# Third-sweep matrix sums made in place, block sums between second-stage pieces, and half buffers stored two steps later, in a four-layer attention and Fourier kernel

## Chip, cores and metric

The kernel runs on one NeuronCore of a Trainium2 chip, as one launch. The metric is the device time of an execution in microseconds (us). Before the change, three runs took 1750.28, 1750.65 and 1752.71 us; their median is 1750.65 us.

## What is computed

A sequence of 2048 rows of 640 numbers passes four layers, twice an attention over eight earlier positions and a Fourier mixing. All of it is float32.

```python
def _B_ref(x, dft_seq_re, dft_seq_im, dft_hid_re, dft_hid_im):
    a = jnp.einsum("bsd,ed->bse", x, dft_hid_re)
    b = jnp.einsum("bsd,ed->bse", x, dft_hid_im)
    y = jnp.einsum("ts,bse->bte", dft_seq_re, a) - jnp.einsum("ts,bse->bte", dft_seq_im, b)
    return y
...
x = A_x
x = x + _A_ref(_layernorm(x, axis=-1), A_wqkv, A_wo)
x = x + _B_ref(_layernorm(x, axis=-1), B_dft_seq_re, B_dft_seq_im, B_dft_hid_re, B_dft_hid_im)
x = x + _A_ref(_layernorm(x, axis=-1), A_wqkv, A_wo)
x = x + _B_ref(_layernorm(x, axis=-1), B_dft_seq_re, B_dft_seq_im, B_dft_hid_re, B_dft_hid_im)
```

`_A_ref` is the attention: 32 heads of 20, a window of 8 positions at distance 2.

## The kernel before, in words

A float32 number is held as a high and a low part, both of a type that TensorE multiplies at its full rate, and a product is three matrix multiplies: high by high, high by low, low by high (`PASSES`). ScalarE (ACT) makes the high part by a cast, VectorE (DVE) the low part by a subtraction, which therefore waits for the cast. The pair is called a half here (`half`, L1517).

The Fourier layers multiply first by the sequence matrices and then by the hidden ones. The first of these steps works on eight column groups: the first two by `run`, the other six as three pairs (t1, t2). A pair uses a scheme with seven block products in place of eight: sums of matrix blocks are multiplied by sums of blocks of x. The Fourier layer after the first attention does its pairs in `pair`. The last layer does them in `pairs7`, which this change is mostly about. There every engine but GpSimd executes in the order in which the code is written (`manual_schedule`), so an instruction that waits holds up all that stand behind it on its engine.

`pairs7` goes through 72 steps: 3 pairs, 3 sweeps, 8 steps. At step n:

- `load(n + 2)` issues three loads of matrix blocks (256 KB each) into a ring of seven buffers (`win`, `xa`), and `loadx(n + 2)` two loads of stored block sums of x (256 KB each, `r<-xc`), all in SyncE's (SP's) DMA queue.
- `atoms(n + 2)` puts the pieces of work that make step n+2's halves into a list. `fill` carries them out as long as fewer than six finished halves are held, so the halves run up to six products ahead of TensorE. A piece is a half, and in the first two sweeps sometimes the sum of two matrix blocks as well (`combine`, L1514, a 128x512 addition on DVE). In those two sweeps a sum stands one piece ahead of the half that needs it.
- the products of the step: 18, 21 and 15 matrix multiplies of 512 columns in a step of the first, second and third sweep.

In the third sweep before the change no sum is made at all: the two sums b22-b12 and b11+b12 that it needs had been made in the other Fourier layer, by `ahead_c` in `pair`, and stored there in the DRAM tensor `ccb` by `keep` (L1862: 48 stores of 256 KB). `pre` (L1490) loads them.

Behind the products of a sweep come, in the later pairs, the pieces of the second stage (`v_stage`, L1431) for the column group that is ready: 9, 12 or 21 multiplies of 320 columns each, and a DVE addition of the result to a half row of x (`half[(j, e)]`, 128x320, L1456). Eight such pieces make one column group: three between or behind the steps of a sweep (1, 0, 6), and five behind the last step of the next sweep (2, 3, 5, 4, 7). They share two PSUM banks, `aux0` and `aux1`; a piece that writes on a bank waits until DVE has added what the piece before left in it. `v_evac` makes the operands of the second stage, and `v_run` carries its parts out one by one in the first steps of a sweep, on ACT and DVE.

The half rows have three buffers (`v_halves`): (0,0) and (0,1) share one. A finished half row is put on a list (`pend`) and stored at the next step (`v_flush`). Matrix sums of the second stage, 24 pieces of 160 KB made in the other Fourier layer, are loaded by `v_get` (`wvb`), one at each step of the first pair's second sweep and two at each step of its third.

Of the kernel before, what the change touches and what calls it, by code (L numbers as in the profile page):

```python
# [10 lines left out]
F32 = mybir.dt.float32  # L11
# [15 lines left out]
P = 128  # L27
# [143 lines left out]
)  # L171
NST = 16
# [8 lines left out]
def tile_layers(ctx: ExitStack, tc: tile.TileContext, x, wqkv, wo, cs, cst, wre, wim, out):  # L181
# [50 lines left out]
    ccb = dr.tile([P, NPAIR, NP, 2, 512], F32, name="ccb")  # L232
# [846 lines left out]
    class LayerB:  # L1079
# [276 lines left out]
        def v_halves(self):  # L1356
            xr = T([P, 2, 320], "xr")
            self.half = {(0, 0): xr[:, 0], (0, 1): xr[:, 0], (1, 0): xr[:, 1], (1, 1): T([P, 320], "qs", bufs=2)}
# [62 lines left out]

        def v_load(self, t, je):
            j, e = je
            nc.sync.dma_start(self.half[je], self.xin[t // 2][:, (t % 2) * 2 + j, e * 320 : (e + 1) * 320])

        def v_flush(self):
            for dst, src in self.pend:
                nc.sync.dma_start(dst, src)
            self.pend = []

        def v_stage(self, t, n, tags=("aux0",) * 3 + ("aux1",)):  # L1431
            chain, prod, plain, (j, e) = STAGES[n]
            start = (t, chain) not in self.vb
            if start:
                self.vb[(t, chain)] = pt([P, 512], tags[chain])
            bank = self.vb[(t, chain)]
            mms = []
            if prod:
                for k in KS:
                    for a, b in PASSES:  # L1440
                        mms.append((self.zv[t][(prod[0], k)][a], self.wv[(prod[1], k)][b]))
            if plain:
                pj, pe = plain
                for k in range(len(KS), KD):
                    for a, b in PASSES:
                        for ri in range(2):
                            w = self.wr[:, b, k] if ri == 0 else self.wi[k][b]
                            mms.append(
                                (self.zp[t][k][:, a, ri, pj * P : (pj + 1) * P], w[:, pe * 320 : (pe + 1) * 320])
                            )  # L1450
            for i, (l, r) in enumerate(mms):
                nc.tensor.matmul(  # L1452
                    bank[:, :320], l, r, start=start and i == 0, stop=i == len(mms) - 1, skip_group_check=not start
                )
            h = self.half[(j, e)]
            nc.vector.tensor_tensor(h, bank[:, :320], h, op=ALU.add)  # L1456
            done = self.vl.setdefault(t, [])
            if (j, e) in done:
                self.pend.append((self.xout[t // 2][:, (t % 2) * 2 + j, e * 320 : (e + 1) * 320], h))
            done.append((j, e))  # L1460

        def pairs7(self):
# [18 lines left out]

            def view():
# [7 lines left out]
            def pre(p, i, n):  # L1490
                tag, bufs = wide[self.nraw % len(wide)]
                self.nraw += 1
                raw = T([P, 2, 256], tag, bufs=bufs) if tag != "win" else wtile([P, 2, 256])
                nc.sync.dma_start(raw.rearrange("p r t -> p (r t)"), ccb[:, p, i, n])
                return raw
# [26 lines left out]
            def atoms(n):  # L1522
# [28 lines left out]
                return [lambda k=k, m=m: half(n, m, raws[n][k]) for k, m in enumerate(("c3", "p12", "c6"))]  # L1551
# [37 lines left out]
            for n, (p, sw, i) in enumerate(steps):  # L1589
# [7 lines left out]
                self.v_flush()  # L1597
# [10 lines left out]
                if sw == 0:  # L1608
                    if i == 0:
                        bk["m5"], bk["m4"], bk["m7"] = banks("m0", "m1"), banks("xt", "t0"), banks("t1", "pq")  # L1610
                    if fast:
                        self.v_run((2, 1, 1, 1, 1, 1, 1, 0)[i])
                        if i == 2:
                            self.v_load(tp, (0, 0))
# [10 lines left out]
                    if fast and i == 4:  # L1625
                        self.v_stage(tp, 1)
                    if i < NP - 1:
                        continue
                    (_, m5s), (m4m, m4s), (dm, ds) = store("stg", CFG["bufs"]["stg"]), store("s2"), store("s3")
# [15 lines left out]
                elif sw == 1:  # L1645
# [3 lines left out]
                    if fast:  # L1649
                        self.v_run((0, 1, 1, 1, 0, 0, 0, 0)[i])  # L1650
                        if i == 4:
                            assert not self.todo
                            self.v_load(tp, (0, 1))
                            self.v_load(tp, (1, 1))
                    p11 = h("p11")
# [18 lines left out]
                    for b in range(2):  # L1674
                        combine(ds[b], z(bk["m1"][b]), ds[b], ALU.add)
                    if fast:
                        for k, st in enumerate((2, 3, 5, 4, 7)):
                            self.v_stage(tp, st)
                            if k in (2, 3):
                                fill(1)  # L1680
                    else:
# [3 lines left out]
                        self.v_halves()  # L1685
                        gets += [("t1", k, b) for k in KS for b in range(2)]
                    self.todo = self.v_evac(t1, (dm, m4m), z(bk["f1"][0]))
                else:
# [3 lines left out]
                    if i == 2:  # L1692
                        self.v_load(t1, (0, 0))
                        self.v_load(t1, (1, 0))
                    if i == 7:
# [10 lines left out]
                    if 3 <= i < 6:  # L1706
                        self.v_stage(t1, (1, 0, 6)[i - 3])
# [10 lines left out]
                    for b in range(2):  # L1718
# [12 lines left out]
            self.v_flush()  # L1731
            self.v_run(9)
            t = NT - 1
            for e in range(2):
                self.half[(0, e)] = wtile([P, 320])
            for je in ((0, 0), (1, 0), (0, 1), (1, 1)):
                self.v_load(t, je)
            for n in (1, 0, 6, 2, 3, 5, 4, 7):
                self.v_stage(t, n, ("m0", "m1", "aux0", "aux1"))
                self.v_flush()  # L1740
# [60 lines left out]
        def pair(self, p, nstats, hooks=None):  # L1801
# [60 lines left out]
            def keep(i, n, raw):  # L1862
                nc.sync.dma_start(ccb[:, p, i, n], raw.rearrange("p r t -> p (r t)"))

            def ahead_c(i):
                b12, b22, b11 = raw(t2, i), raw(t2, NP + i), raw(t1, i)
                x6 = self.x_slot(6, i, ring)
                keep(i, 0, combine(b22, b12, b22, ALU.subtract))
                c3 = split(b22)

                def rest():
                    keep(i, 1, combine(b11, b11, b12, ALU.add))
                    return split(b11)

                return x6, c3, split(b12), rest
# [204 lines left out]
```

## Time and profile before

| | before |
|---|---|
| median of three runs | 1750.65 us |
| the profiled execution, its time | 1748.35 us |
| its span, first to last instruction | 1746.6 us |
| DVE busy over the span | 1370.6 us (78%) |
| ACT busy over the span | 834.9 us (48%) |
| `pairs7`, from its first product to the end | 1315.9 to 1746.6 us |
| DRAM written | 103.75 MB |

The profile lists each engine's instructions with their line in the kernel. "PE" is TensorE, "SPq" SyncE's DMA queue. In a row of the time line the first number is the start in us from the start of the span, the second the length, and what stands in brackets is the idle time of that engine just before and what ended it. A line of the helper `combine` is L1515, the cast and the subtraction of a half are L1519 and L1520; a product is L1574 and a second-stage multiply L1452.

The third sweeps of the three pairs begin at 1405.27, 1549.60 and 1683.21 us.

### The profile page before, as it was taken

What the parts mean: (1) busy time and instruction counts of PE and PEld (TensorE: products, weight loads), DVE (VectorE), ACT (ScalarE), POOL (GpSimd) and SP (SyncE); (2) the same over time, 40 slices, a digit from 0 to 9 for tenths busy, and PEclk for the clock granted to TensorE, in tenths of its full rate; (3) what the DMA queues carried; (4) which work ended last, traced back from release to release, by engine and by line L of the source; (5) the groups of instructions that cost most, each with busy time, mean ns of one, the idle gap of its engine ahead of it and who ended that gap; (6) DMA issues with size and microseconds to landing.
All of it is one profiled execution on the core that took longest, in us unless ns stands there. A gap on an engine that the chain in (4) does not pass through costs nothing.

```text
span 1746.6 us, 26782 instructions
## 1 busy us (share of the span) xinstructions
PE 1712.0 (98%) x8771; PEld 1489.9 (85%) x8771; DVE 1370.6 (78%) x2166; ACT 834.9 (48%) x1838; POOL 614.7 (35%) x570
## 2 busy tenths in 40 slices
PE   9999999999999999999999999999999998999999
PEld 7889898878888888888888888988888887888888
DVE  5999999978778767767649988899787657767765
ACT  5655645554454444445524444555434433444441
POOL 4899999930000000000029988899100000000000
PEclk9999999999999999999999999999999999999999
DMA  7777779859899788878757856798587887787772
GB/s 253 260 228 258 217 242 313 327 195 355 290 338 328 256 262 284 263 262 267 235 157 256 271 190 204 237 352 296 194 316 255 286 261 253 255 269 244 252 267 77
DMA packets 297499, 450.74 MB, mean 258 GB/s; under 512 B 32240, under 2 KB 169840, under 8 KB 297104
## 3 DMA queue, kind: packets, MB, share of 16 engines
q1 hardware_dynamic: 283184, 439.36, 75.2%
q10 hardware_dynamic: 14176, 9.67, 1.8%
q8 instruction: 70, 1.15, 0.3%
q14 instruction: 69, 0.57, 0.1%
HBM read 345.18 MB, written 103.75 MB: 257 GB/s over the span
## 4 chain that ended last, share of the span: by engine, by line
PE 72%; DMA 10%; DVE 10%; issue 3%; ACT 3%; POOL 2%; SPq 1%; ACTq 0%; DVEq 0%; POOLq 0%
PE m L512 19%; PE aux L1248 7%; PE aux L675 6%; PE t L1574 5%; PE m L1574 5%; PE aux L1452 4%; PE m L1793 3%; DMA win<-cs_in 3%; PE t L1793 3%; PE m L1181 3%; PE pq L1574 3%; PE t L1181 3%; PE xt L1574 2%; PE xt L1793 2%; PE xt L1181 1%
## 5 line engine op out<-in xcount | busy, mean ns | idle before, releaser
L512 PE MATMUL m<-r,s 128*128 128x512 f32 (+1 forms) x1890 | 421.8, 379 | 0.2 <-ACT sg L527 0.2
L512 PEld LDWEIGHTS m<-r,s 128*128 128x128 f32 x1890 | 344.6, 188 | 54.6 <-ACT sg L527 1.5
L592 DVE TENSOR_TENSOR pr<-pq,win 128x1280 f32<-128x1280 f32 x128 | 189.8, 1483 | 36.8 <-PE aux L1248 20.3
L650 POOL TENSOR_TENSOR pr<-pr 128x640 f32<-128x640 f32 x126 | 207.5, 1647 | 28.5 <-DVE pr L635 27.3
L595 POOL TENSOR_TENSOR pr<-pr 128x640 f32<-128x640 f32 x123 | 176.5, 1435 | 88.0 <-DVE pr L592 87.8
L635 DVE TENSOR_TENSOR pr<-pq,win 128x1280 f32<-128x1280 f32 x128 | 190.4, 1488 | 2.6
L313 POOL TENSOR_TENSOR stats<-stats,mhalf 128x1 f32<-128x1 f32 (+1 forms) x26 | 18.9, 728 | 448.7 <-ACT stats L307 448.7
L1248 PE MATMUL aux<-r2a,zo 128*128 128x320 f32 x480 | 141.4, 309 | 0.0
L1248 PE MATMUL aux<-pr,zo 128*128 128x320 f32 x440 | 130.1, 309 | 0.0
L651 POOL TENSOR_TENSOR pr<-pr 128x320 f32<-128x320 f32 x126 | 112.7, 895 | 9.9
L605 DVE TENSOR_REDUCE lg<-pr 128x64 f32<-128x640 f32 (+1 forms) x128 | 107.2, 837 | 11.3 <-POOL pr L595 11.1
L1786 ACT CAST r<-win 128x512 fp32r<-128x512 f32 x126 | 76.2, 619 | 76.3 <-DVE win L1822 49.5
L1181 PE MATMUL m<-s,r 128*128 128x512 f32 x348 | 107.1, 396 | 2.9 <-DMA s<-c0b 0.9
L1181 PE MATMUL t<-s,r 128*128 128x512 f32 x348 | 105.2, 391 | 0.0
L1519 ACT CAST r<-win 128x512 fp32r<-128x512 f32 x111 | 68.8, 622 | 75.9 <-PE pq L1574 15.0
L1520 DVE TENSOR_TENSOR r<-win,r 128x512 fp32r<-128x512 f32 x111 | 76.4, 690 | 30.4 <-ACT r L1519 29.7
L1787 DVE TENSOR_TENSOR r<-win,r 128x512 fp32r<-128x512 f32 x126 | 84.8, 688 | 19.4 <-ACT r L1786 18.6
L526 ACT COPY stg<-m 128x480 f32<-128x480 f32 x96 | 53.5, 557 | 94.0 <-PE m L512 88.2
L1248 PEld LDWEIGHTS aux<-r2a,zo 128*128 128x128 f32 x480 | 90.1, 188 | 1.4
L1248 PEld LDWEIGHTS aux<-pr,zo 128*128 128x128 f32 x440 | 82.6, 188 | 1.6
L675 PE MATMUL aux<-r2a,ot 128*128 128x320 f32 x540 | 83.7, 310 | 0.0
L675 PEld LDWEIGHTS aux<-r2a,ot 128*128 128x128 f32 x540 | 80.4, 188 | 1.5 <-ACT wa L498 0.3
(450 smaller groups left out, 3816.9 us busy)
## 6 DMA issues: line engine op xcount, KB each, us to landing
win<-cs_in SPq DMA_DIRECT2D x314, 256.0 KB
r<-xc SPq DMA_DIRECT2D x264, 256.0 KB
win<-kvb SPq DMA_DIRECT2D x96, 440.0 KB
xa<-cs_in SPq DMA_DIRECT2D x104, 256.0 KB
win<-kvb SPq DMA_DIRECT2D x64, 360.0 KB
xc<-sg SPq DMA_DIRECT2D x28, 512.0 KB
kvb<-stg SPq DMA_DIRECT2D x33, 320.0 KB
qs<-qb SPq DMA_DIRECT2D x64, 160.0 KB
```

Source lines behind the costliest of these rows:

```text
L512: nc.tensor.matmul(mt[g][:, : GW[q]], st[:, a, k], wq[q][:, b, k], start=n == 0, stop=n == 14)
L592: nc.vector.tensor_tensor(pr, q, wview(u, jp, 0, [[1, FE]]), op=ALU.mult)
L595: nc.gpsimd.tensor_tensor(pv[:, :, 0:10], pv[:, :, 0:10], pv[:, :, 10:20], op=ALU.add)
L605: nc.vector.tensor_reduce(rows(lgs[u], jp), pv.rearrange("p (a h) d -> p a h d", h=HE), axis=AX.X, op=ALU.add,)
L635: nc.vector.tensor_tensor(pr.rearrange("p j w (h d) -> p (j w) h d", d=DH), rows(lgs[u], jp).unsqueeze(3).to_broadcast([P, 2 * W, HE, DH]) ...
L650: g.tensor_tensor(pr[:, :, 0:4], pr[:, :, 0:4], pr[:, :, 4:8], op=ALU.add)
L651: g.tensor_tensor(pr[:, :, 0:2], pr[:, :, 0:2], pr[:, :, 2:4], op=ALU.add)
L675: nc.tensor.matmul(m[:, :320], oT[(c, j)][:, a, k], wo_s["w"][:, b, k, e * 320 : (e + 1) * 320], start=(i, k) == (0, 0), stop=(i, k) == (2 ...
L1181: self.last = nc.tensor.matmul(self.z[t][k], self.xn[c][:, a, j, k * P : (k + 1) * P], self.ct[s][:, b], start=s == 0 and i == 0, stop=s = ...
L1248: self.last = nc.tensor.matmul(self.ym[e][:, :320], zt[(k, a, ri)][:, j2 * P : (j2 + 1) * P], w[:, e * 320 : (e + 1) * 320], start=(k, a, ...
L1574: nc.tensor.matmul(bank, w(a, kb), h[b], start=start and (a, b) == (0, 0) and not cont, stop=stop and (a, b) == (1, 0), skip_group_check=cont,
L1793: nc.tensor.matmul(bank, w(a, kb), hl[b], start=start and (a, b) == (0, 0), stop=stop and (a, b) == (1, 0),)
```

## The change

It has five parts.

1. `ccb`, `keep` and `pre` are gone. The other Fourier layer no longer stores the sums; the third sweep of `pairs7` loads three plain blocks in each step and makes both sums itself (`c0`, `c2`).
2. `v_get` begins in the first pair's first sweep: 8, 10 and 6 loads in its three sweeps (`GETS`) in place of 0, 8 and 16.
3. Each half row has a buffer of its own; (1,1) is split over spare columns of two tiles (two DVE additions of 160 columns in place of one of 320). A finished one is stored two steps later.
4. Two of the block sums behind the last step of a second and third sweep move to places between the second-stage pieces; in the last pair's third sweep they stay.
5. Piece 1 of the second stage moves one step later in the first sweep, pieces 1, 0 and 6 one step later in the third.

```diff
+GETS = ((0, 1, 1, 1, 1, 1, 1, 2), (2, 2, 1, 1, 1, 1, 1, 1), (0, 0, 1, 1, 1, 1, 1, 1))
...
-            self.half = {(0, 0): xr[:, 0], (0, 1): xr[:, 0], (1, 0): xr[:, 1], (1, 1): T([P, 320], "qs", bufs=2)}
+            self.half = {
+                (0, 0): [(xr[:, 0], 0, 320)],
+                (1, 0): [(xr[:, 1], 0, 320)],
+                (0, 1): [(T([P, 320], "qs", bufs=2), 0, 320)],
+            }
+            self.spares(spare)
+
+        def spares(self, spare):
+            self.half[(1, 1)] = [(m[:, 4, :160], 160 * i, 160 * i + 160) for i, m in enumerate(spare)]
...
-            h = self.half[(j, e)]
-            nc.vector.tensor_tensor(h, bank[:, :320], h, op=ALU.add)
...
+            for h, c0, c1 in self.half[(j, e)]:
+                nc.vector.tensor_tensor(h, bank[:, c0:c1], h, op=ALU.add)
+                if (j, e) in done:
+                    self.pend.append((self.now + 2, self.v_row(self.xout, t, (j, e), c0, c1), h))
...
-                    raws[n] = [pre(p, i, 0), self.s_raw(t2, i, wide), pre(p, i, 1)]
+                    raws[n] = [self.s_raw(*a, wide) for a in ((t2, NP + i), (t2, i), (t1, i))]
...
-                return [lambda k=k, m=m: half(n, m, raws[n][k]) for k, m in enumerate(("c3", "p12", "c6"))]
+
+                def c0():
+                    b22, b12, _ = raws[n]
+                    combine(b22, b12, b22, ALU.subtract)
+                    half(n, "c3", b22)
+
+                def c2():
+                    _, b12, b11 = raws[n]
+                    combine(b11, b11, b12, ALU.add)
+                    half(n, "c6", b11)
+
+                return [c0, lambda: half(n, "p12", raws[n][1]), c2]
...
-                if p == 0 and sw > 0:
-                    for _ in range((0, 1, 2)[sw]):
-                        if gets:
-                            self.v_get(*gets.pop(0))
+                self.now = n
+                self.v_flush(n)
+                if p == 0:
+                    for _ in range(GETS[sw][i]):
+                        self.v_get(*gets.pop(0))
...
-                    if 3 <= i < 6:
-                        self.v_stage(t1, (1, 0, 6)[i - 3])
+                    if 4 <= i < 7:
+                        self.v_stage(t1, (1, 0, 6)[i - 4])
...
-                    for b in range(2):
-                        combine(es[b], z(bk["m1"][b]), es[b], ALU.add)
-                    self.v_run(9)
+                    if last:
+                        for b in range(2):
+                            combine(es[b], z(bk["m1"][b]), es[b], ALU.add)
+                    assert not self.todo
...
                         if last:
                             self.v_run(2 if k < 3 else 1)
+                        elif k < 2:
+                            combine(es[k], z(bk["m1"][k]), es[k], ALU.add)
...
-                keep(i, 0, combine(b22, b12, b22, ALU.subtract))
-                c3 = split(b22)
...
+                c3 = split(combine(b22, b12, b22, ALU.subtract))
```

On DVE, in the second pair's third sweep at steps 1 and 2, where the halves for steps 3 and 4 are made, the order before is this (L1520 is the low part of a half, L1390 and L1391 are the part of `v_evac` that stands between two steps, `r`, `s` the halves, `win`, `xa` the matrix blocks):

```order
L1520 TENSOR_TENSOR r_2_1750_12162<-xa_15481,r_2_1750_12162 128x2x256
L1520 TENSOR_TENSOR r_3_1803_12512<-win_15483,r_3_1803_12512 128x2x256
L1520 TENSOR_TENSOR r_3_1803_12512<-win_15485,r_3_1803_12512 128x2x256
L1390 TENSOR_TENSOR zo_2159_15439<-s_2111_14996,zo_2159_15439 128x128
L1391 TENSOR_TENSOR wa_13425<-s_2111_14996,wa_13425 128x256
L1520 TENSOR_TENSOR s_2176_15536<-win_15514,s_2176_15536 128x512
```

After the change the same place on DVE reads as follows (L1525 is `combine`, L1530 the low part of a half, L1398 and L1399 the part of `v_evac`):

```order
L1525 TENSOR_TENSOR xa_15457<-win_15459,xa_15457 128x512
L1530 TENSOR_TENSOR r_2_1750_12113<-xa_15457,r_2_1750_12113 128x2x256
L1530 TENSOR_TENSOR r_3_1803_12463<-win_15459,r_3_1803_12463 128x2x256
L1525 TENSOR_TENSOR win_15461<-win_15461,win_15459 128x512
L1530 TENSOR_TENSOR r_3_1803_12463<-win_15461,r_3_1803_12463 128x2x256
L1398 TENSOR_TENSOR zo_2159_15417<-s_2111_14967,zo_2159_15417 128x128
L1399 TENSOR_TENSOR wa_13376<-s_2111_14967,wa_13376 128x256
L1525 TENSOR_TENSOR win_15497<-win_15499,win_15497 128x512
```

Two sums have come in, and each stands directly ahead of the low part that is made from its own result; in between, ACT has to cast that result.

Behind the last step of the same sweep DVE has, before, six block sums (`stg`, `s` from the banks `xt`, `t`, `m`) and then the additions to the half rows (`xr`, `qs` from `aux`):

```order
L1515 TENSOR_TENSOR stg_15362<-xt_15454,stg_15362 128x512
L1515 TENSOR_TENSOR s_2112_14997<-xt_15454,stg_14995 128x512
L1515 TENSOR_TENSOR stg_15362<-t_2167_15455,stg_15362 128x512
L1515 TENSOR_TENSOR s_2112_14997<-t_2167_15455,stg_14995 128x512
L1515 TENSOR_TENSOR stg_15362<-m_2118_15051,stg_15362 128x512
L1515 TENSOR_TENSOR stg_15362<-m_2119_15052,stg_15362 128x512
L1456 TENSOR_TENSOR xr_14225<-aux_2187_15640,xr_14225 128x320
L1456 TENSOR_TENSOR qs_14226<-aux_2201_15794,qs_14226 128x320
L1456 TENSOR_TENSOR xr_14225<-aux_2187_15640,xr_14225 128x320
```

After the change the same stretch of DVE is this:

```order
L1525 TENSOR_TENSOR stg_15337<-xt_15429,stg_15337 128x512
L1525 TENSOR_TENSOR s_2112_14968<-xt_15429,stg_14966 128x512
L1525 TENSOR_TENSOR stg_15337<-t_2167_15430,stg_15337 128x512
L1525 TENSOR_TENSOR s_2112_14968<-t_2167_15430,stg_14966 128x512
L1469 TENSOR_TENSOR qs_14192<-aux_2190_15666,qs_14192 128x320
L1525 TENSOR_TENSOR stg_15337<-m_2118_15021,stg_15337 128x512
L1469 TENSOR_TENSOR s_2111_14967<-aux_2201_15785,s_2111_14967 128x160
L1469 TENSOR_TENSOR s_2112_14968<-aux_2201_15785,s_2112_14968 128x160
L1525 TENSOR_TENSOR stg_15337<-m_2119_15022,stg_15337 128x512
L1469 TENSOR_TENSOR xr_14191<-aux_2190_15666,xr_14191 128x320
```

The two sums from the banks `m` have moved behind the first and the second addition, so the first addition stands behind four sums in place of six.

More of the change, by code (lines that the diff above doesn't have):

```diff
@@ L1420, in v_run, with v_row, v_flush @@
                     fn(*args)
+        def v_row(self, x, t, je, c0, c1):
+            j, e = je
+            return x[t // 2][:, (t % 2) * 2 + j, e * 320 + c0 : e * 320 + c1]
         def v_load(self, t, je):
[L1423 to L1427, printed above, removed]
+            for h, c0, c1 in self.half[je]:
+                nc.sync.dma_start(h, self.v_row(self.xin, t, je, c0, c1))
+        def v_flush(self, n):
+            while self.pend and self.pend[0][0] <= n:
+                _, dst, src = self.pend.pop(0)
                 nc.sync.dma_start(dst, src)
-            self.pend = []
         def v_stage(self, t, n, tags=("aux0",) * 3 + ("aux1",)):
@@ L1480, in store, with wider @@
                 return m, [m[:, b] for b in range(2)]
+            def wider(tag):
+                m = T([P, 5, 256], tag)
+                d = m[:, :4].rearrange("p (b r) t -> p b r t", b=2)
+                return m, d, [d[:, b] for b in range(2)]
             def view():
@@ L1730, in pairs7 @@
                         self.todo = self.v_evac(t2, (dm, em), fr)
-            self.v_flush()
+            self.v_flush(n)
             self.v_run(9)
             t = NT - 1
[L1734 to L1737, printed above, removed]
+            for j in range(2):
+                for e in range(2):
+                    self.half[(j, e)] = [(wtile([P, 320]), 0, 320)]
+                    self.v_load(t, (j, e))
             for n in (1, 0, 6, 2, 3, 5, 4, 7):
+                self.now += 1
+                self.v_flush(self.now)
                 self.v_stage(t, n, ("m0", "m1", "aux0", "aux1"))
-                self.v_flush()
+            self.v_flush(self.now + 2)
         def x_whole(self, side, i):
```

44 lines of the change are left out of this document (17 added, 27 removed).

## Prediction

> **What bounds the kernel now.** The page comes first: TensorE is busy in 98% of the span, so only time in which it stands still or runs slowly can be won, about 35 us in all.
>
> ```profile
> span 1746.6 us, 26782 instructions
> PE 1712.0 (98%) x8771; PEld 1489.9 (85%) x8771; DVE 1370.6 (78%) x2166; ACT 834.9 (48%) x1838; POOL 614.7 (35%) x570
> ```
>
> Next, the waits of PE from 1240 us to the end, where `pairs7` lies (total, times, longest):
>
> ```profile
> PE aux L1452 <- DVE xr L1456: 6.4, 4, 3.7
> PE aux L1452 <- DMA r2a<-wvb: 3.2, 1, 3.2
> PE xt L1574 <- DMA r<-xc: 3.1, 2, 1.6
> ```
>
> These are 12.7 us. PE's time line puts them in place. The rows below are the start of the first pair's third sweep and the pieces behind it, then the second pair's third sweep with its pieces 2, 3 and 5 and the start of the next sweep, then the last pair.
>
> ```profile
> 1405.27 0.86 PE L1574 MATMUL xt<-r,r 128*128 128x512 f32 x3
> ...
> 1453.88 2.23 PE L1452 MATMUL aux<-r,zo 128*128 128x320 f32 x7 [3.67 <-DVE xr L1456]
> 1456.44 2.24 PE L1452 MATMUL aux<-pr,zo 128*128 128x320 f32 x9
> ...
> 1462.04 1.32 PE L1574 MATMUL m<-r,r 128*128 128x512 f32 x5
> ...
> 1549.60 0.86 PE L1574 MATMUL xt<-s,r 128*128 128x512 f32 x3
> ...
> 1577.54 0.86 PE L1574 MATMUL xt<-s,r 128*128 128x512 f32 x3
> ...
> 1580.97 0.84 PE L1574 MATMUL xt<-r,r 128*128 128x512 f32 x3
> ...
> 1584.37 1.48 PE L1452 MATMUL aux<-r,zo 128*128 128x320 f32 x9
> 1585.68 1.48 PE L1452 MATMUL aux<-r2a,zo 128*128 128x320 f32 x9
> 1589.39 1.29 PE L1452 MATMUL aux<-r,zo 128*128 128x320 f32 x7 [2.23 <-DVE xr L1456]
> ...
> 1595.65 1.55 PE L1574 MATMUL m<-s,r 128*128 128x512 f32 x6
> ...
> 1683.21 0.86 PE L1574 MATMUL xt<-r,r 128*128 128x512 f32 x3
> ...
> 1717.97 1.48 PE L1452 MATMUL aux<-r,zo 128*128 128x320 f32 x9
> ...
> 1720.60 1.19 PE L1452 MATMUL aux<-r,zo 128*128 128x320 f32 x7
> ```
>
> A step of the third sweep takes PE 3.43 us (1577.54 to 1580.97), the sweep 34.8 us (1549.60 to 1584.37), and pieces 2 and 3 take 2.6 us more, so piece 5 could start 37.4 us after the sweep's start. It starts after 39.8 us in the second pair, 48.6 us in the first (from 1405.27) and 37.4 us in the last. The multiplies at 1456.44 take 2.24 us for nine, those at 1584.37 1.48 us: the clock has fallen. The rows by stage say so too (PE, PEld, DVE, ACT, POOL busy, granted clock, DMA share, GB/s):
>
> ```profile
> 1315.90:1349.70 33.80, 33.13 (x147) 27.14 (x146) 26.67 (x42) 15.10 (x26) 0.00 (x0) 1.00 0.86 284
> ...
> 1396.60:1405.30 8.70, 8.70 (x62) 8.70 (x61) 3.54 (x7) 1.45 (x3) 0.00 (x0) 1.00 0.03 13
> 1405.30:1443.80 38.50, 35.45 (x174) 29.96 (x174) 21.75 (x40) 15.45 (x27) 0.00 (x0) 1.00 0.99 322
> 1443.80:1462.20 18.40, 11.48 (x62) 10.74 (x61) 11.11 (x19) 3.75 (x7) 0.00 (x0) 0.81 0.53 190
> ```
>
> From 1453.88 to the next sweep at 1462.04 the first pair takes 8.16 us, the second 6.26 (1589.39 to 1595.65): **1.9 us lost to the clock**, after two idles of 3.2 and 3.7 us close together. The single 2.23 us cost no clock.
>
> **The two new sums in each step of the third sweep** decide. Each stands on DVE directly ahead of the low part of its own half, which waits for ACT's cast of the sum. The other Fourier layer has the same three instructions, of the same size:
>
> ```profile
> 641.36 0.69 DVE L1822 TENSOR_TENSOR xa<-win,xa 128x512 f32<-128x512 f32 x1
> 642.82 0.69 DVE L1787 TENSOR_TENSOR s<-xa,s 128x512 fp32r<-128x512 f32 x1 [0.76 <-ACT s L1786]
> 643.42 0.68 DVE L1787 TENSOR_TENSOR s<-win,s 128x512 fp32r<-128x512 f32 x1
> ...
> 645.39 0.69 DVE L1787 TENSOR_TENSOR r<-win,r 128x512 fp32r<-128x512 f32 x1
> 646.12 0.69 DVE L1822 TENSOR_TENSOR win<-xa,win 128x512 f32<-128x512 f32 x1
> ```
>
> and on ACT:
>
> ```profile
> 642.16 0.62 ACT L1786 CAST s<-xa 128x512 fp32r<-128x512 f32 x1 [1.56 <-DVE xa L1822]
> ```
>
> From the sum's start to the low part's start are 1.46 us (641.36 to 642.82), 0.76 of them idle. Low part to low part is 0.60 (642.82 to 643.42), low part to a sum 0.73 (645.39 to 646.12), 0.13 more. I take **1.55 us of DVE per sum** (1.46 and most of the 0.13). The bounds are 0.60, if something filled the wait, and 1.59. Nothing can fill it where DVE keeps the written order, unless the cast came earlier, and the cast needs the sum. A step then takes DVE 3 x 0.60 + 2 x 1.55 = 4.9 us against PE's 3.43: from the third step on, PE waits for halves.
>
> How late DVE is at the end follows from its busy time in the second pair's third sweep:
>
> ```profile
> 1549.70:1584.40 34.70, 34.70 (x173) 29.92 (x172) 25.39 (x46) 17.81 (x31) 0.00 (x0) 1.00 0.88 295
> ...
> 1683.40:1718.00 34.60, 34.60 (x172) 29.83 (x172) 22.96 (x43) 14.35 (x25) 0.00 (x0) 1.00 0.66 220
> ```
>
> Six halves, two steps' worth, are made before the sweep begins, in the idle of the sweep before; so 12 of the 16 sums fall inside. DVE needs 25.4 + 12 x 1.55 + 0.2 (its start) = 44.2 us. Then come four block sums and the first addition (the first row is the last thing that DVE does there ahead of a sum):
>
> ```profile
> 1550.81 0.68 DVE L1396 TENSOR_TENSOR ot<-pq,ot 128x512 fp32r<-128x512 f32 x1
> ...
> 1585.26 0.68 DVE L1515 TENSOR_TENSOR stg<-xt,stg 128x512 f32<-128x512 f32 x1
> 1585.86 0.68 DVE L1515 TENSOR_TENSOR s<-xt,stg 128x512 f32<-128x512 f32 x1
> ...
> 1588.85 0.48 DVE L1456 TENSOR_TENSOR xr<-aux,xr 128x320 f32<-128x320 f32 x1
> ```
>
> That is 4 x 0.60 + 0.5, so piece 5 starts after 47.1 us in place of 39.8: **second pair +7.3 us**. The two sums moved behind save 1.2 us here, already in it; the block of sums is no longer the limit, the halves ahead of it are.
>
> *Last pair.* There are no halves of a next sweep: the 22.96 us hold 2.6 us of the block sums, leaving 20.4. So 20.4 + 18.6 + 0.2 = 39.2, then six sums (3.6) and 0.5: 43.3 us in place of 37.4, **+5.9**. DVE then trails through the last `v_evac`; for that I take 0.6 (between 0 and 1.2, two sums' length).
>
> *First pair.* Its sweep starts with its blocks still on the way:
>
> ```profile
> 1410.64 1.37 DVE L1520 TENSOR_TENSOR r<-win,r 128x512 fp32r<-128x512 f32 x2 [3.47 <-ACT r L1519]
> ```
>
> and SP's waits say why: the store of the half row stands ahead of the loads.
>
> ```profile
> SPq L1268 <- DVE xr L1261: 7.7, 1, 7.7
> ```
>
> This store is not touched, and DMA is at 0.03 of its share until 1405.30. The second low part there begins at 1411.3, its cast 0.66 earlier, so a sum that needs both blocks can start at about 1410.7, 5.4 us into the sweep; in the second pair it follows the `v_evac` parts that end at 1551.5, 1.9 us in. So 47.1 + 3.5 = 50.6 us in place of 48.6, +2.0; the 1.9 us of the clock would go: **+0.1**. So the waits that the earlier `v_get` and the lighter third sweep remove (r2a 3.2, r<-xc at most 3.1) come back as waits for DVE.
>
> **The other parts.** Pieces behind the second sweeps: the four waits of 6.4 us hold 3.67 and 2.23, and two of 0.25 remain, which the moved sums cover: -0.5. The 48 stores in the other layer lie beside PE work; that layer's waits for DVE are
>
> ```profile
> PE m L1793 <- DVE r L1787: 1.4, 2, 1.0
> ```
>
> so -1.0 (0 to -1.4). In the first pair's first sweep eight loads of 160 KB are 1.3 MB, 4 us at 322 GB/s; its DMA share of 0.86 leaves about that (0.14 of 33.8 us is 4.7), so 0, at most +4 where the sweep is one load late. Half buffers and later stores: SP's waits for them end no PE wait, 0; without the moved order the loads behind them come up to two steps (7 us) later, which the lead of two steps still covers. The 160-column additions cost 0.1 us a piece, 0.
>
> **The clock.** PE now stands still for some 5.5 us ahead of piece 5 in the first two pairs (PE is 4 to 5 us late by then, reaches the wait at about 41.7 and leaves it at 47.1). 2.23 us cost no clock, 6.9 in two parts did. I take one fall of 1.9 us for the two places; the bounds are none and two.
>
> [...]
>
> Sum against the profiled execution's 1748.35 us: 0.1 + 7.3 + 5.9 + 0.6 - 0.5 - 1.0 + 1.9 = +14.3, so 1762.7. The median of the runs stands 2.3 us above that execution, so **1765 us**.
>
> **Rivals.** (1) *The sums fit*: DVE fills the wait, or the sums run ahead. Then DVE needs 25.4 + 12 x 0.60 + 0.2 = 32.8 us, less than PE's 34.8, and the waits go: first pair -10.3 (3.2 + 3.7 + 1.9, and half of 3.1), second -2.2, others -1.5: 1736.6 us. For it speaks that DVE is idle for 9 of 34.7 us; against it that this idle is in the order, not in the amount. (2) *A draw*: at a price w per sum the three starts of piece 5 are 28.5 + 12w, 32 + 12w and 24.7 + 12w against 39.8, 50.5 (clock included) and 37.4. With -1.5 they balance at w = 1.22 us. 1.46 was measured, so DVE would have to win a quarter of a us per sum elsewhere: 1750 us. (3) *Both clocks fall*: 1767 us. (4) *Early matrix sums starve the first sweep*: +4, 1769 us. That the change does not do what it says is excluded by the order of DVE, which shows the sums.
>
> **Numbers.** My case 0.67, rival 1 0.15, rival 2 0.08, rivals 3 and 4 0.05 each. Less than 0.2%, 3.5 us, can't be told from no change here: faster 0.15, same 0.08, slower 0.77. My case alone goes from 1759 (w = 1.46, no clock fall) to 1769 (w = 1.59, two falls). The range takes in rivals 2 to 4, and the slower side of their bounds: 1746 to 1775; rival 1 is left out.
>
> **What would show it.** Right: in the third sweeps DVE idle by ACT's cast about 0.75 us behind each sum, 16 per pair; PE waits at L1574's line for DVE's halves from step 3 on, 4 to 5 us a sweep; one wait of about 5 us ahead of piece 5 in the first two pairs, about 1 us in the last; no wait for r2a. Wrong: a third sweep of 35 us in the second pair, or a DVE that is idle waiting for PE there.

## The result and the profile after

The changed kernel takes 1767.24 us (median of four runs, 1766.98 to 1770.74); the kernel before, run beside it, takes 1750.47. The ratio is 1.0102, with a 95% interval from 1.0082 to 1.0122: **slower by 1%**. The profiled execution took 1767.22 us; its span is 1765.4 us against 1746.6.

The page's first lines, of the changed kernel:

```profile
span 1765.4 us, 26771 instructions
PE 1723.2 (98%) x8771; PEld 1490.9 (84%) x8771; DVE 1397.7 (79%) x2224; ACT 833.1 (47%) x1838; POOL 615.0 (35%) x570
```

PE has as many multiplies as before and counts as busy 11 us longer: at half clock a multiply takes longer (nine 2.15 us below, for 1.48), and one that starts by itself counts for more than one in a row (0.49 us at 1566.81 below; three in a row take 0.86). At a granted clock of 1.00 a multiply of the parts takes 0.23 us in a row in the kernel before (512 columns, six in 1.55 us at 1595.65), one of bf16 there 0.22 us (512 columns, eight in 1.89 us at 4.16). DVE has 27 us more to do, little beside 1765. What ends PE's waits from 1240 us to the end (total, times, longest):

```profile
PE aux L1464 <- DVE qs L1469: 11.6, 5, 4.3
PE xt L1595 <- DMA r<-xc: 1.8, 1, 1.8
PE aux L1464 <- DVE xr L1469: 1.4, 2, 0.7
PE m L1595 <- DVE r L1530: 1.1, 5, 0.2
...
PE xt L1595 <- DVE r L1530: 0.9, 4, 0.2
```

L1464 is now the second stage's multiply, L1469 its addition, L1595 a product, L1525 `combine`, L1529 the cast and L1530 the low part of a half. The waits for r2a are gone and those for r<-xc are 1.3 us less; waits for DVE have taken their place. PE's time line shows where: the end of the second pair's second sweep, then its third sweep with pieces 2, 3, 5 and 4.

```profile
1546.02 1.31 PE L1464 MATMUL aux<-r,zo 128*128 128x320 f32 x7 [1.19 <-DVE qs L1469]
...
1552.29 0.86 PE L1595 MATMUL xt<-s,r 128*128 128x512 f32 x3
...
1566.81 0.49 PE L1595 MATMUL xt<-s,r 128*128 128x512 f32 x1 [0.47 <-ACT s L1529]
1567.54 0.73 PE L1595 MATMUL xt<-s,r 128*128 128x512 f32 x2 [0.23 <-DVE s L1530]
...
1591.29 1.47 PE L1464 MATMUL aux<-r,zo 128*128 128x320 f32 x9
1593.45 1.58 PE L1464 MATMUL aux<-r2a,zo 128*128 128x320 f32 x9 [0.69 <-DVE xr L1469]
1599.37 2.24 PE L1464 MATMUL aux<-r,zo 128*128 128x320 f32 x7 [4.34 <-DVE qs L1469]
...
1601.94 2.15 PE L1464 MATMUL aux<-pr,zo 128*128 128x320 f32 x9
```

The sweep now takes 39.0 us (1552.29 to 1591.29) in place of 34.8, in small waits for halves. Piece 5 starts 47.1 us after the sweep's start, where it was 39.8, and nine multiplies then take 2.15 us for 1.48: the clock has fallen (0.50 from 1596.61 to 1603.42 us). DVE in that sweep shows the cause:

```profile
1559.93 0.69 DVE L1525 TENSOR_TENSOR xa<-win,xa 128x512 f32<-128x512 f32 x1
1561.43 0.69 DVE L1530 TENSOR_TENSOR r<-xa,r 128x512 fp32r<-128x512 f32 x1 [0.82 <-ACT r L1529]
1562.04 0.69 DVE L1530 TENSOR_TENSOR r<-win,r 128x512 fp32r<-128x512 f32 x1
1562.64 0.68 DVE L1525 TENSOR_TENSOR win<-win,win 128x512 f32<-128x512 f32 x1
1564.15 0.69 DVE L1530 TENSOR_TENSOR r<-win,r 128x512 fp32r<-128x512 f32 x1 [0.82 <-ACT r L1529]
```

with ACT's casts of the two sums:

```profile
1560.78 0.62 ACT L1529 CAST r<-xa 128x512 fp32r<-128x512 f32 x1 [1.60 <-PE t L1595]
...
1563.49 0.62 ACT L1529 CAST r<-win 128x512 fp32r<-128x512 f32 x1 [1.57 <-DVE win L1525]
```

The profile puts the start of the first cast down to PE, but both casts start 0.85 us after their sum's start, and the second waits for DVE by the profile too. After each sum DVE stands idle for 0.82 us until ACT has cast that sum. From sum to low part are 1.50 us (1559.93 to 1561.43). Over the sweep, the costliest groups of DVE (busy, mean ns, idle before and what ended it) say that this idle is nearly all there is:

```profile
L1530 DVE TENSOR_TENSOR r<-win,r 128x512 fp32r<-128x512 f32 x7 | 4.8, 690 | 4.1 <-ACT r L1529 4.1
L1530 DVE TENSOR_TENSOR s<-win,s 128x512 fp32r<-128x512 f32 x6 | 4.0, 688 | 2.5 <-ACT s L1529 2.5
L1530 DVE TENSOR_TENSOR r<-xa,r 128x512 fp32r<-128x512 f32 x5 | 3.5, 691 | 3.3 <-ACT r L1529 3.3
L1525 DVE TENSOR_TENSOR win<-win,win 128x512 f32<-128x512 f32 x5 | 3.4, 685 | 0.0
```

9.9 us of idle, twelve times 0.82, though DVE is the engine that PE waits for.

The span's 18.8 us, cut at the starts of the sections on PE (us; a sweep runs to its first piece behind, the pieces to the next sweep):

| section | before | after | difference |
|---|---|---|---|
| start to the first product of `pairs7` | 1315.95 | 1315.30 | -0.65 |
| first pair, third sweep and pieces | 38.37 + 18.40 | 42.73 + 16.44 | +2.4 |
| second pair, pieces behind the second sweep | 9.30 | 10.26 | +0.96 |
| second pair, third sweep and pieces | 34.76 + 11.28 | 38.99 + 16.16 | +9.1 |
| last pair, pieces behind the second sweep | 9.31 | 10.26 | +0.95 |
| last pair, third sweep and the rest on PE | 34.76 + 25.22 | 38.99 + 27.23 | +6.2 |

These come to 19.0; all other sections up to PE's last multiply are the same to 0.1 us, and what follows it is 0.1 us shorter. The first row can't be put down to the change: in the changed kernel and the six experiments with the same code ahead of `pairs7`, its first product starts between 1311.7 and 1316.6 us.

### The profile page after: what moved, and what is told of

Read it like the earlier page. It is cut to its first block, busy times and chain, and to the rows that moved or that the text cites. A ratio compares the mean times of both kernels' runs of the same rounds, so it can differ in the third digit from the quotient of the medians.

```text
span 1765.4 us, 26771 instructions
## 1 busy us (share of the span) xinstructions
PE 1723.2 (98%) x8771; PEld 1490.9 (84%) x8771; DVE 1397.7 (79%) x2224; ACT 833.1 (47%) x1838; POOL 615.0 (35%) x570
## 4 chain that ended last, share of the span: by engine, by line
PE 79%; DVE 9%; DMA 6%; ACT 3%; issue 2%; POOL 0%; SPq 0%; ACTq 0%; DVEq 0%
PE m L512 23%; PE aux L1248 9%; PE aux L675 7%; PE m L1824 4%; PE t L1824 4%; PE m L1181 4%; PE t L1595 4%; PE t L1181 3%; PE aux L1464 3%; PE m L1595 3%; PE pq L1595 3%; PE xt L1824 2%; PE pq L1824 2%; PE xt L1595 2%; PE xt L1181 2%
## 5 line engine op out<-in xcount | busy, mean ns | idle before, releaser
L1529 ACT CAST r<-win 128x512 fp32r<-128x512 f32 x111 | 68.1, 621 | 96.5 <-DVE win L1525 50.8
L1530 DVE TENSOR_TENSOR r<-win,r 128x512 fp32r<-128x512 f32 x111 | 76.0, 690 | 33.1 <-ACT r L1529 32.9
```

## The experiments

The forecast's reason is called the **order theory**: what costs is that a sum stands directly ahead of the low part of its own half, so that DVE waits for ACT. Its rivals: the **work theory** (sixteen more additions per pair are too much for DVE) and the **load theory** (the other loads delay the blocks). The first four kernels were timed beside the kernel before, at 1752.28 us there; the next four beside it at 1752.09; the changed kernel was timed beside it at 1750.47. So a difference below between two kernels of different rounds may be off by some 2 us.

### Each sum one piece ahead of its half

The changed kernel, with the third sweep's halves in another order, so that as many sums are made, each with another half's low part between it and its own. The products take the halves in the same order.

```diff
                 def c0():
                     b22, b12, _ = raws[n]
                     combine(b22, b12, b22, ALU.subtract)
-                    half(n, "c3", b22)
+                    half(n, "p12", b12)
-                def c2():
-                    _, b12, b11 = raws[n]
+                def c1():
+                    b22, b12, b11 = raws[n]
                     combine(b11, b11, b12, ALU.add)
-                    half(n, "c6", b11)
-                return [c0, lambda: half(n, "p12", raws[n][1]), c2]
+                    half(n, "c3", b22)
+                return [c0, c1, lambda: half(n, "c6", raws[n][2])]
...
```

> The changed kernel, but in the third sweep a sum stands one piece ahead of the half that needs it, as in the other two sweeps: the halves are made in the order p12, c3, c6, the products of a step go in that order too, and DVE has sum, low part of p12, sum, low part of c3, low part of c6. The sums, their number, the loads and all else are those of the changed kernel. Order theory (each sum costs 1.5 us because DVE waits 0.82 us for the cast of its result): the wait is gone, a step needs 5 x 0.60 = 3.0 us of DVE against PE's 3.43, so the second pair's third sweep falls from 39.0 to 34.8 to 35.5 us, the wait of 4.3 us ahead of piece 5 to under 1.2, both falls of the clock go; in all 1737 to 1743 us, faster than both kernels. Work theory (16 more additions in a sweep are too much for DVE, in whatever order): as the changed kernel, 1763 to 1769. Load theory (the third sweep is late through its loads and stores, not through the sums): also 1763 to 1769.

1740.85 us (1738.32 to 1741.56), ratio 0.9934 (0.9911 to 0.9956). DVE in the second pair's third sweep:

```profile
1548.30 0.68 DVE L1525 TENSOR_TENSOR xa<-win,xa 128x512 f32<-128x512 f32 x1
1548.90 0.68 DVE L1530 TENSOR_TENSOR r<-win,r 128x512 fp32r<-128x512 f32 x1
1549.51 0.68 DVE L1525 TENSOR_TENSOR win<-win,win 128x512 f32<-128x512 f32 x1
1550.11 0.68 DVE L1530 TENSOR_TENSOR r<-xa,r 128x512 fp32r<-128x512 f32 x1
1551.01 0.69 DVE L1530 TENSOR_TENSOR r<-win,r 128x512 fp32r<-128x512 f32 x1 [0.22 <-ACT r L1529]
```

and its groups over that sweep:

```profile
L1530 DVE TENSOR_TENSOR r<-win,r 128x512 fp32r<-128x512 f32 x9 | 6.2, 686 | 0.7 <-ACT r L1529 0.7
...
L1530 DVE TENSOR_TENSOR s<-win,s 128x512 fp32r<-128x512 f32 x7 | 4.8, 685 | 0.0
L1530 DVE TENSOR_TENSOR r<-xa,r 128x512 fp32r<-128x512 f32 x5 | 3.4, 686 | 0.2 <-ACT r L1529 0.2
```

As many DVE instructions and the same loads: the idle behind ACT falls from 9.9 to 0.9 us, the sweep takes 35.2 us, near the 34.8 before the change, and the kernel is 26.4 us faster than the changed one by the medians (28 us, each measured against the kernel before beside it). This refutes the work and the load theory as causes of the loss. The order accounts for more than the whole loss: the rest of the change is a gain.

### The kept sums put back

The changed kernel, with `ccb`, `keep` and `pre` back: no sums in the third sweep.

```diff
+    ccb = dr.tile([P, NPAIR, NP, 2, 512], F32, name="ccb")
...
-                    raws[n] = [self.s_raw(*a, wide) for a in ((t2, NP + i), (t2, i), (t1, i))]
+                    raws[n] = [pre(p, i, 0), self.s_raw(t2, i, wide), pre(p, i, 1)]
...
```

> The changed kernel with the kept sums put back (48 stores in the other Fourier layer, third sweep loads them and makes none); the half buffers, the later stores, the earlier loads of the second stage's sums, the moved block sums and pieces stay. Order theory: no sum waits, third sweep of the second pair 34.8 us, wait ahead of piece 5 at most 1.2, no fall of the clock, 1737 to 1743 us: what the other four parts of the change are worth by themselves, 8 to 13 us less than before the change. Work theory: the same, since the work is gone. Load theory (loads, stores and the other parts make the loss): 1757 or more.

1745.68 us (1740.64 to 1749.38, ten runs), ratio 0.9957 (0.9944 to 0.9970). The profiled execution, with 1741.28, is among the fastest of a wide spread; the median lies 3 us above the expected range, and the gain on the kernel before is 6.6 us, not the 8 to 13 expected. What fills the other runs no profile shows. In the one there is, PE waits for stored sums of x, which with both sums ahead cost 0.5 us:

```profile
PE aux L1465 <- DVE qs L1470: 4.6, 2, 2.6
PE xt L1592 <- DMA r<-xc: 2.5, 2, 1.3
```

So the change's other parts gain on the kernel before. Sums made in place, well ordered, are 4.8 us better than kept ones by the medians, but the intervals of the two ratios overlap, and in the two profiled executions PE's part of `pairs7` takes 419.1 and 419.6 us: that they are better is not shown.

### The sums alone in the kernel before

The mirror image: the kernel before, with only part 1 of the change.

```diff
-                    raws[n] = [pre(p, i, 0), self.s_raw(t2, i, wide), pre(p, i, 1)]
+                    raws[n] = [self.s_raw(*a, wide) for a in ((t2, NP + i), (t2, i), (t1, i))]
...
-                return [lambda k=k, m=m: half(n, m, raws[n][k]) for k, m in enumerate(("c3", "p12", "c6"))]
+                return [c0, lambda: half(n, "p12", raws[n][1]), c2]
...
```

> The kernel before with part 1 of the change alone: kept sums gone, the third sweep makes them in place, each directly ahead of its own half. Order and work theory: third sweeps of the second and last pair 38.5 to 39.5 us with the waits of the sums 0.82 us each; the block sums that stay together add 1.2 us ahead of piece 5 in the first two pairs; 1766 to 1774 us, at least as slow as the whole change. Load theory: within 4 us of the kernel before, 1747 to 1755.

1772.67 us (1771.68 to 1774.90), ratio 1.0120 (1.0101 to 1.0139), as expected. The second and last pair's third sweeps take 39.2 us. PE's waits:

```profile
PE aux L1451 <- DVE xr L1455: 15.4, 5, 6.4
...
PE aux L1451 <- DMA r2a<-wvb: 1.9, 1, 1.9
```

Here all six block sums still stand ahead of the pieces: the longest wait is 6.4 us where the changed kernel has 4.3, with 0.7 ahead of the piece before it. The wait for r2a stays, shorter (1.9 for 3.2).

### The sums behind the low part

As many additions of the same size, the same loads and the products in the order of the changed kernel, but each sum stands behind the low part. The halves are made from the plain blocks, so this leaves the sums out of the products.

```diff
-                    combine(b22, b12, b22, ALU.subtract)
                     half(n, "c3", b22)
+                    combine(b22, b12, b22, ALU.subtract)
...
```

> The changed kernel, but each sum of the third sweep stands directly behind the low part of the half that ought to be made from it, so the halves are made from the plain blocks and the sums go nowhere: this leaves the sums out of the products. Number and size of the additions, the loads and the order of the products are those of the changed kernel; only the wait of the cast for the sum is gone. Order theory: as with the sum one piece ahead, 1737 to 1743 us, the second pair's third sweep 34.8 to 35.5. Work theory and load theory: 1763 to 1769, third sweep near 39.

1739.87 us (1739.51 and 1740.23), ratio 0.9931 (0.9904 to 0.9958): the same as with the sums ahead, by another way of taking the wait out. DVE's amount of work is not what costs.

### One of the two sums ahead

```diff
-                def c2():
+                def c1():
                     _, b12, b11 = raws[n]
                     combine(b11, b11, b12, ALU.add)
-                    half(n, "c6", b11)
-                return [c0, lambda: half(n, "p12", raws[n][1]), c2]
+                    half(n, "p12", b12)
+                return [c0, c1, lambda: half(n, "c6", raws[n][2])]
```

> Dose: the changed kernel, with only the sum of the sixth product one piece ahead of its half; the sum of the third product stays directly ahead of its own. Order theory (a sum directly ahead of its half costs DVE 1.55 us, a sum with a piece between 0.60): DVE needs 25.4 + 6 x 1.55 + 6 x 0.60 + 0.2 = 38.5 us for the second pair's third sweep, and piece 5 starts 41.4 us after the sweep's start (47.1 in the changed kernel, about 38.5 with both sums ahead); in all 6 to 7 us above the kernel with both ahead: 1745 to 1750 us. If instead only the number of sums or of loads counted, it would be as the changed kernel: 1767. If one moved sum were enough (the wait counts only from a threshold that one sum does not reach): 1741, as with both ahead.

1755.91 us (1750.21 to 1763.37, ten runs), ratio 1.0029 (1.0016 to 1.0043): between the two orders, but 6 us above the expected range; the profiled execution, the fastest, lies at its upper end, and what makes the other nine 4 to 13 us slower no profile shows. In the profiled one, piece 5 of the second pair starts 42.9 us after the sweep's start (41.4 expected). The third low part of a step waits there too, 0.22 us for the cast ahead of it; four such waits are 0.9 of the 1.5 us more. Piece 5 comes only 3.1 us later than in the kernel before, but PE stands at four places:

```profile
PE aux L1464 <- DVE qs L1469: 10.3, 4, 4.3
PE xt L1595 <- DMA r<-xc: 1.9, 1, 1.9
```

The granted clock over its span is 0.997, with both sums ahead 1.0. It is 0.50 from 1410.10 to 1413.50 us, and behind piece 5's wait in the second pair a single multiply takes 0.47 us (at 1588.26) where it takes 0.31 with both ahead. The direction follows the order theory; the price per sum does not carry over to the whole time: waits at the second sweeps' ends (1.19 us twice) and the clock were not in the sum, and most of the spread stays open.

### The block sums back in one block

Both sums ahead, and part 4 of the change undone.

```diff
-                    if not fast:
-                        for b in range(2):
-                            combine(ds[b], z(bk["m1"][b]), ds[b], ALU.add)
+                    for b in range(2):
+                        combine(ds[b], z(bk["m1"][b]), ds[b], ALU.add)
...
-                            if k < 2:
-                                combine(ds[k], z(bk["m1"][k]), ds[k], ALU.add)
...
```

The same is done with the two sums of the third sweep.

> Both sums ahead of their halves, and the block sums that the change put between the pieces put back ahead of them. If those moves are worth what their place says: two sums, 1.2 us, later at piece 5 in the first two pairs, 0.25 at each of two second sweeps' ends, so 2.9 us above 1741: 1743 to 1746, and up to 1748 if the clock falls in the first pair (its wait would be 2.5 + 1.2 = 3.7 us). If DVE's block is hidden anyway: 1741.

1748.27 us (1746.21 to 1754.71, ten runs), ratio 0.9974 (0.9959 to 0.9990): 7.4 us above the kernel with both sums ahead, more than the 2.9 expected. The profiled execution is the slowest of the ten, 6.4 us above their median, so its rows show more than the usual cost. The granted clock over its span is 0.996, with the moves 1.0; five multiplies of piece 5 in the second pair take 1.70 us, where all seven take 1.31 with the moves. Piece 5 of the second pair waits 4.54 us there (1.10 with the moves). Only 1.2 of the 3.4 more are the two sums, by their length. DVE's waits in the sweep ahead hold the rest:

```profile
1558.83 0.69 DVE L1525 TENSOR_TENSOR win<-win,win 128x512 f32<-128x512 f32 x1 [0.99 <-DMA win<-cs_in]
...
1565.34 0.69 DVE L1525 TENSOR_TENSOR win<-xa,win 128x512 f32<-128x512 f32 x1 [1.34 <-DMA xa<-cs_in]
...
1566.97 0.69 DVE L1525 TENSOR_TENSOR win<-win,xa 128x512 f32<-128x512 f32 x1 [0.28 <-DMA win<-cs_in]
...
1584.52 0.69 DVE L1530 TENSOR_TENSOR r<-win,r 128x512 fp32r<-128x512 f32 x1 [1.12 <-ACT r L1529]
```

The blocks cost 2.61 us there; with the moves the first two waits are 0.74 and 0.64 us and the others are not there. So 1.2 more are blocks that come late and 1.1 is a wait for ACT. The waits at the second sweeps' ends came as 1.34 us each, not as 0.25. That these loads are later because DVE gave their buffers free later is a reading of the rows; no run here separates it.

### The matrix sums loaded late

Both sums ahead, and part 2 of the change undone.

```diff
-GETS = ((0, 1, 1, 1, 1, 1, 1, 2), (2, 2, 1, 1, 1, 1, 1, 1), (0, 0, 1, 1, 1, 1, 1, 1))
+GETS = ((0,) * 8, (1,) * 8, (2,) * 8)
```

> Both sums ahead of their halves, and the matrix sums loaded as in the kernel before (none in the first sweep, one a step in the second, two in the third). If the early loads are what removed the wait for r2a: a wait of 1 to 3 us for r2a comes back ahead of a piece of the first pair, part of it beside the wait of 2.5 us for DVE that is there already: 1741 to 1746. If the kept sums' absence alone removed it: no wait for r2a, 1741 or a little less, since the first sweep carries fewer loads.

1746.80 us (1745.72 to 1750.44, ten runs), ratio 0.9974 (0.9964 to 0.9984): 6 us slower than with early loads, 0.8 above the expected range. The wait for r2a is back, ahead of the last three multiplies of a piece of the first pair:

```profile
1448.74 1.00 PE L1464 MATMUL aux<-r2a,zo 128*128 128x320 f32 x3 [2.31 <-DMA r2a<-wvb]
1452.07 2.24 PE L1464 MATMUL aux<-r,zo 128*128 128x320 f32 x7 [2.33 <-DVE qs L1469]
```

It does not lie beside the wait for DVE but adds to it, and the two together cost the clock (2.24 us for seven multiplies): the first pair's pieces take 16.4 us, 11.6 with early loads. The sweep ahead of them takes 39.6 us, 37.3 with early loads. At 1415.84 us DVE waits 1.52 us for a matrix block there (0.66 with early loads), PE 1.48 us for the cast behind it, and the clock falls once more (0.51 from 1419.20 to 1422.60 us). That the late loads hold up this block is a reading; no run separates it.

### All block sums between the pieces

Both sums ahead, and in the first two pairs the four other block sums of the third sweep between the pieces as well, so that no addition of a piece stands behind the block.

```diff
-                    for b in range(2):
+                    def m3_sums(b):
                         combine(es[b], z(bk["m3"][b]), es[b], ALU.add)
                         combine(ds[b], z(bk["m3"][b]), m5s[b], ALU.add)
...
                         elif k < 2:
+                            m3_sums(k)
                             combine(es[k], z(bk["m1"][k]), es[k], ALU.add)
```

> Both sums ahead of their halves, and in the first two pairs all six block sums of the third sweep stand between the pieces, three behind piece 2 and three behind piece 3. If piece 5 waits only because the first addition stands behind four block sums, the waits of 2.5 and 1.1 us go and at most 0.5 comes back at piece 4: 1738 to 1740. If it waits for the halves themselves (DVE late from the sweep): no change, 1741.

**1737.33 us** (1734.87 to 1738.94), ratio 0.9919 (0.9904 to 0.9933): the lowest median here, 30 us below the changed one and 0.7 below the expected range. It is 3.5 us below the kernel with both sums ahead, but the intervals of the two ratios overlap. Pieces 2, 3, 5 and 4 of the second pair:

```profile
1573.88 1.48 PE L1464 MATMUL aux<-r,zo 128*128 128x320 f32 x9
1575.19 1.48 PE L1464 MATMUL aux<-r2a,zo 128*128 128x320 f32 x9
1576.51 1.19 PE L1464 MATMUL aux<-r,zo 128*128 128x320 f32 x7
...
1578.20 1.58 PE L1464 MATMUL aux<-pr,zo 128*128 128x320 f32 x9 [0.21 <-DVE s L1469]
```

Piece 5 no longer waits; piece 4 waits 0.21. In the first pair 0.39 and 0.65 us are left of 2.52, and the granted clock over the span is 1.0. So with both sums ahead, piece 5 had waited for the block of sums ahead of its addition and not for the halves.

## Why the prediction was right, point by point

The forecast, 1765 us, is 2 us below the median. That it is so close is in part luck: the sum, 14.3 us on the profiled execution, falls 4.7 us short, and the 2.3 us added because the median before stood above that execution made up for half of it; the changed kernel's median (1767.24) and profiled execution (1767.22) are the same. The mechanism came as forecast. Term by term, by the table of sections:

- **The price of a sum** was put at 1.55 us and measured as 1.50. The 0.13 us more between a low part and a sum did not appear in the sweep (0.60 from 1562.04 to 1562.64). The wait is 0.82 us, a little above the 0.76 of the other layer. Over twelve sums 1.55 is 0.6 us too much; still, the block sums begin 44.15 us after the second pair's sweep starts (44.2 forecast), so DVE had some 0.5 us of other work and waits that the sum did not hold.
- **Piece 5's start** came out as worked out: 50.8 us after the sweep's start in the first pair (50.6 forecast), 47.1 in the second (47.1), 42.6 in the last (43.3). Twelve of the 16 sums inside a sweep was the right count: twelve idles of 0.82 us in the second pair.
- **Second pair**: 7.3 and 1.9 for the clock forecast, 9.1 measured. **Last pair**: 6.5 forecast with the trailing end, 6.2 measured (piece 5 5.2 us later, not 5.9; the end 1.0, not 0.6). **The other layer**: -1.0 forecast; the -0.65 of the table lies within what this section varies by with the same code, so this term is not shown. **The 160-column additions**: two take 0.55 us (1599.83), one of 320 columns 0.48 (1598.84), so 0.07 more a piece for 0.1 forecast.
- **First pair**, mis-sized: +0.1 forecast, +2.4 measured. The clock's 1.9 us were taken as gone, since one fall was allowed for two places. It fell at both (0.50 from 1453.25 to 1460.06 and from 1596.61 to 1603.42 us). That is the condition of rival 3, priced at 1767, so its clock came true and not the one of the forecast. The time line of PE in the first pair has the same seven multiplies at half clock (2.23 us) as the second:

```profile
1404.61 0.86 PE L1595 MATMUL xt<-r,r 128*128 128x512 f32 x3
...
1455.44 2.23 PE L1464 MATMUL aux<-r,zo 128*128 128x320 f32 x7 [4.02 <-DVE qs L1469]
```

- **The second sweeps' ends**, with the wrong sign: -0.5 forecast, +1.9 measured. The step said that two waits of 0.25 us would be covered by the moved sums. But the same paragraph on the halves had four of the 16 sums made there, ahead of the third sweep; their waits make DVE late for the first additions (1.19 us at 1546.02). With both sums ahead these pieces take 9.19 us; with part 1 alone 11.44; with the kept sums back 8.79, 0.5 less than before the change at each of the two ends. So the moved sums do save time there, but less than the waits of the new sums cost. The sums made ahead were counted only as a saving inside the sweep.

The last two together miss by 4.7 us, and they explain the sum, 19.0 measured against 14.3. One figure of the forecast does not follow from its conditions: with w = 1.46 and no fall of the clock its own sum gives 1760, with w = 1.59 and two falls 1768, where it has 1759 and 1769.

The cause is shown twice, by the sums moved ahead and by the sums moved behind. What two parts of the change are worth without it is shown as well: with both sums ahead, the early matrix loads are worth 6.0 us and the moved block sums 7.4. These numbers do not add up in other settings. With the kept sums back all other parts together gain 6.6 us on the kernel before. In the changed kernel, where DVE is late anyway, they are worth some 4 us: part 1 alone costs 20.4, the whole change 16.8. The half buffers with their later stores and the moved pieces (parts 3 and 5) were not taken out by themselves.

## What to carry to other kernels

When a value goes from one engine to another and back, and both keep the written order, count the way there and back, not only the operations: here an addition of 0.60 us cost 1.50, because nothing stood between it and the instruction that waited for its cast. Before an engine is called too slow for added work, see what its idle time waits for; if that is the echo of its own result, put another piece's work in between. Such idle costs only where another engine waits for this one: with the kept sums back, DVE is idle behind ACT for 7.4 us in the second pair's third sweep, and the sweep takes 35.2 us. A loss of this kind can hide gains of other parts, so time the parts one by one before a change is dropped whole.

## What was not expected of the hardware

The length of an idle did not decide whether the clock fell. The rows by stage (PE, PEld, DVE, ACT, POOL busy, granted clock, DMA share, GB/s) around the wait ahead of piece 5 in the first pair, with the sums behind (an idle of 2.45 us):

```profile
1443.50:1446.90 3.40, 0.95 (x6) 0.69 (x5) 3.40 (x7) 0.43 (x1) 0.00 (x0) 1.00 0.99 339
1446.90:1450.30 3.40, 3.40 (x14) 3.40 (x14) 2.37 (x6) 0.62 (x1) 0.00 (x0) 0.50 0.10 38
```

and with the sums ahead (2.52 us):

```profile
1444.30:1447.70 3.40, 1.65 (x12) 1.39 (x10) 3.37 (x6) 0.89 (x2) 0.00 (x0) 1.00 0.98 346
1447.70:1451.10 3.40, 2.63 (x18) 2.64 (x19) 3.37 (x8) 0.62 (x1) 0.00 (x0) 1.00 0.27 103
```

Behind the shorter idle the granted clock was 0.50 in the row of 3.4 us, behind the longer one 1.00. With one sum ahead a row at 0.50 came behind a single idle of 1.85 us:

```profile
1406.70:1410.10 3.40, 1.54 (x7) 1.01 (x6) 2.56 (x5) 2.43 (x5) 0.00 (x0) 1.00 0.86 259
1410.10:1413.50 3.40, 3.40 (x10) 2.62 (x9) 1.80 (x5) 0.92 (x3) 0.00 (x0) 0.50 1.07 388
```

Nor do PE's busy times ahead put the cases in order. In the rows of 3.4 us they are 0.95 and 1.54 us ahead of these two falls and 1.65 where none came; but with the matrix sums late 1.94 us, in short pieces, stand ahead of a fall (1415.80 to 1419.20 us at 1.00, the next 3.40 us at 0.51). What decides whether the clock falls is not shown here.

The prediction has the clock of the kernel before fall after two idles of 3.2 and 3.7 us. It fell at 1451.30 us (0.50 from there to 1458.12), only 1.1 us into the second idle, so most of that idle came after the fall. The 3.4 us ahead of it hold three multiplies:

```profile
1447.90:1451.30 3.40, 0.97 (x3) 0.48 (x3) 3.37 (x6) 1.50 (x3) 0.00 (x0) 1.00 1.02 371
```
